# Per-head KV column tiles, `wo` folded in 32x32 tiles, re-paced first keys, and later modulation rows spread through DRAM, in an adaLN block with linear attention and SwiGLU

## The chip, the cores and the metric

The kernel runs on one core of one Trainium2 chip. The metric is the device time of one execution in microseconds (us). The engines: PE is TensorE's matmul, PEld its weight load, DVE is VectorE, ACT is ScalarE, POOL is GpSimd, SPq is the queue of SyncE.

## The reference, cut to what matters

```python
x = A_x                                            # [1, 2048, 1024] bf16
mod = (silu(c) @ w_mod).reshape(1, 6, 1, -1)       # six rows of 1024
sa, ca, ga, sb, cb, gb = mod[:, 0], ..., mod[:, 5]
h = layernorm(x) * (1 + ca) + sa
# attention: q, k, v = h @ wqkv, 32 heads of 32; pq, pk = phi(q), phi(k)
kv = einsum('bhsd,bhse->bhde', pk, v);  z = sum_s pk
o = (pq @ kv) / (pq . z + 1e-6)                    # per head
x = x + ga * (o @ wo)
h = layernorm(x) * (1 + cb) + sb
x = x + gb * ((silu(h @ w_gate) * (h @ w_up)) @ w_down)   # 1024 -> 3584 -> 1024
```

## The kernel before

The sequence is cut in four chunks (`sc`) of 512 rows. Per chunk TensorE makes keys, values and queries from `hT`, the transposed and modulated layernorm. The products of keys and values (KV) are summed over the chunks, and then each head's 32x32 block of KV is multiplied into `wo` ("folded"), so that queries need only one product. All this is the first 185 us; gate/up and down follow.

```python
def mm(out, lhsT, rhs, start, stop):       # lhsT is loaded as weights, rhs moves
    return tc.keep_in_program_order(nc.tensor.matmul(out, lhsT=lhsT, rhs=rhs, start=start, stop=stop))
def keep_warm(acc, n):                     # filler matmuls on zeros, for the clock
    for _ in range(n):
        mm(acc[:], lhsT=sel[:, 0, :], rhs=sel[:], start=True, stop=True)

def kv_phase(sc):                          # four heads at once: 128x128, off-diagonal blocks masked later
    for hg0 in range(0, HG, 3):
        ...
            for t in range(STC):
                mm(kvv[:, i, :], lhsT=pks[sc][:, t, (hg0 + i) * P:(hg0 + i + 1) * P],
                   rhs=vs[sc][:, t, hg0 + i, 0:P + 1], start=(t == 0), stop=(t == STC - 1))
        ... # vector: copy or add into kv_acc

def mod_rows(blks):                        # rows ga, gb (chunk 2) or sb, cb (chunk 3): 32 matmuls in four column tiles
    ...
def mod_bc(row):                           # chunk 2: spread ga, gb over the partitions
    for g in range(4):
        mm(ps[:], lhsT=sel[:, g, :], rhs=row[:], start=True, stop=True); ...
def mod_cols(row):                         # chunk 3: sb, cb as columns
    ... # 16 matmuls of one column

# first keys of chunk 0 (b: half of the columns, q=1: scale ca, q=0: shift sa)
pe_transpose_tile(hT, xns[0], 0, DC);  keep_warm(spare, 1)
mod_block(0, 1, 0, 4)
pe_transpose_tile(hT, xns[1], 1, DC);  keep_warm(spare, 1)
pe_transpose_tile(hT, xns[2], 2, DC // 2);  keep_warm(spare, 3)
mod_block(0, 0, 0, 2)
...                                        # modulate, mod_block(0, 0, 2, 4), modulate
k_mms(0, gs, accs, 0, 3)
...
k_mms(0, gs7, accs7, 0, 4)
mod_block(1, 0, 0, 2)
for cc in (4, 5): modulate(hT, cc, ca1T, saT)

# the fold, spread between query groups
for hg, nb in wf[3 * (qc - 5):3 * (qc - 4)]:
    ps = acc_b("wf")
    w = wo[hg // 4][:, hg % 4, nb * NB:(nb + 1) * NB]
    mm(ps[:], lhsT=KVT[:, hg, :], rhs=w, start=True, stop=True)
    nc.scalar.copy(out=w, in_=ps[:])
```

## Time and profile before

| | before |
|---|---|
| first timing, median of 3 | 844.36 us |
| span of the profile | 841.5 us |
| PE busy | 833.8 us, 99% |
| KV phase, four of them | 1.81 us each (1.91 ahead of the rows) |
| KV transposes | 0.54 us |
| broadcast (`bcr`) and column (`mcol`) matmuls of the later rows | 0.87 and 0.41 us |

From the page of the kernel before: the busy table's line of PE, the row of the granted clock in tenths over 40 slices, and the chain of work that ended last.

```profile
PE 833.8 (99%) x4289; PEld 385.5 (46%) x4289; DVE 306.8 (36%) x599; ACT 176.2 (21%) x268; POOL 55.6 (7%) x163
...
PEclk9999999999999999999999999999999999999999
...
PE 98%; DMA 1%; SPq 0%; DVE 0%; issue 0%
```

TensorE is what there is to shorten. Its waits, all of them (view of waits, PE: total us, times, longest):

```profile
PE mod_ps L98 <- DMA wme<-in_w_mod_dram: 1.8, 1, 1.8
PE acc L98 <- DVE sel L412: 1.2, 1, 1.2
PE acc L98 <- DVE hT L221: 0.7, 1, 0.7
PE mod_ps L98 <- DVE saT L267: 0.2, 1, 0.2
```

The timeline of PE in the kernel before (start us, busy us, line, tiles, shapes, count). A matmul's busy time includes its latency (379 ns for 512 columns, which start 216 ns apart), so a group's cost is the distance from its start to the start of the next line.

```profile
14.78 4.06 PE L98 MATMUL acc<-wk,hT 128*128 128x512 bf16 x18
...
31.86 13.98 PE L98 MATMUL acc<-wv,hT 128*128 128x512 bf16 x64
...
62.94 1.98 PE L98 MATMUL kvp<-v,pk 128*128 128x129 bf16 x32
64.75 10.52 PE L98 MATMUL acc<-wk,hT 128*128 128x512 bf16 x48
...
161.69 0.61 PE L101 MATMUL tp<-ident,kvs 128*128 128x128 bf16 x8
162.23 0.63 PE L98 MATMUL den<-pq,Zden 128*32 128x128 bf16 x32
...
166.25 0.81 PE L98 MATMUL wf<-wo,kvs 128*128 128x512 bf16 x3
...
183.52 13.98 PE L98 MATMUL a_ps<-wo,pq 128*128 128x512 bf16 x64
```

The `den` line is the model for what the change does to KV: "128*32" is a matmul in a column tile of 32, and 32 of them, each of 128 moving columns, need 0.56 us.

### The profile page before, as it was taken

The page shows a single profiled execution, that of the slowest core. Times are in us where ns is not written, and L with a number is a line of the kernel's source. Part 1 is how long each engine was busy: PE and PEld are TensorE (multiplying, and loading weights), DVE is VectorE, ACT ScalarE, POOL GpSimd, SP SyncE. Part 2 cuts the span into 40 slices and gives each one's busy share as a digit, 9 for nine tenths or more (in the row PEclk, how much of TensorE's full clock was granted, in tenths as well). Part 3 has the DMA queues.
Part 4 walks back from the last instruction along what each step waited for, and adds up shares of the span by engine and source line. Part 5 has one row for each costly group of instructions (what it writes and reads, how often), then busy time and mean ns, then how long its engine had stood idle before and what let it go on. Part 6 is the DMA issues. An engine that isn't in the chain of part 4 may idle for free.

```text
span 841.5 us, 10528 instructions
## 1 busy us (share of the span) xinstructions
PE 833.8 (99%) x4289; PEld 385.5 (46%) x4289; DVE 306.8 (36%) x599; ACT 176.2 (21%) x268; POOL 55.6 (7%) x163
## 2 busy tenths in 40 slices
PE   8999999999999999999999999999999999999998
PEld 4444444544444444444444444444444444444444
DVE  5656563467523324432221344211124432111122
ACT  3355353354211111101111010111110101111000
POOL 3011010112050001100000010000001100000000
PEclk9999999999999999999999999999999999999999
DMA  9895770029998545528434073581504629720011
GB/s 304 308 248 122 232 188 1 2 52 250 348 236 251 193 145 175 154 70 257 151 100 150 25 233 106 178 260 52 198 1 131 182 69 315 238 66 1 17 60 50
DMA packets 127232, 128.74 MB, mean 153 GB/s; under 512 B 33616, under 2 KB 108880, under 8 KB 126672
## 3 DMA queue, kind: packets, MB, share of 16 engines
q1 hardware_dynamic: 123600, 115.36, 45.7%
q0 software_dynamic: 3584, 12.72, 4.9%
q8 instruction: 33, 0.54, 0.3%
q14 instruction: 15, 0.12, 0.1%
HBM read 108.01 MB, written 12.71 MB: 143 GB/s over the span
## 4 chain that ended last, share of the span: by engine, by line
PE 98%; DMA 1%; SPq 0%; DVE 0%; issue 0%
PE acc L98 89%; PE a_ps L98 7%; DMA wme<-in_w_mod_dram 1%; PE kvp L98 1%; PE modr L98 0%; PE wf L98 0%; PE mod_ps L98 0%; PE den L98 0%; SPq L120 0%; PE tp L101 0%; PE bcr L98 0%; SPq L131 0%; SPq L125 0%; DVE hT L221 0%; PE mcol L98 0%
## 5 line engine op out<-in xcount | busy, mean ns | idle before, releaser
L98 PE MATMUL acc<-h2T,wgu 128*128 128x512 bf16 x1792 | 387.6, 379 | 0.0
L98 PEld LDWEIGHTS <-wgu 128*128 128x128 bf16 x1792 | 175.0, 98 | 211.6
L98 PE MATMUL acc<-wd,gu 128*128 128x512 bf16 (+2 forms) x924 | 196.1, 373 | 0.0
L591 DVE TENSOR_TENSOR gu<-acc,e 128x512 bf16<-128x512 f32 x112 | 77.5, 692 | 299.3 <-PE acc L98 296.5
L590 ACT ACTIVATE e<-acc 128x512 f32<-128x512 f32 x112 | 66.9, 597 | 374.8 <-PE acc L98 374.8
L98 PEld LDWEIGHTS <-gu 128*128 128x128 bf16 x924 | 89.2, 98 | 104.6
L98 PEld LDWEIGHTS <-hT 128*128 128x128 bf16 x512 | 49.4, 98 | 60.3 <-DVE hT L221 1.3
L612 DVE TENSOR_TENSOR e<-acc,gb_bc 128x512 f32<-128x512 f32 (+2 forms) x33 | 22.3, 676 | 131.3 <-PE acc L98 131.3
L98 PE MATMUL acc<-wk,hT 128*128 128x512 bf16 x256 | 57.6, 379 | 0.7 <-DVE hT L221 0.7
L98 PE MATMUL a_ps<-wo,pq 128*128 128x512 bf16 x256 | 57.4, 379 | 0.0
L98 PE MATMUL acc<-hT,wq 128*128 128x512 bf16 x256 | 57.1, 379 | 0.0
L98 PE MATMUL acc<-wv,hT 128*128 128x512 bf16 x256 | 55.9, 379 | 0.0
L273 ACT ACTIVATE eb<-acc 128x512 bf16<-128x512 f32 x64 | 37.9, 596 | 63.4 <-PE acc L98 60.3
L218 ACT ACTIVATE xn<-x,nmr,rstd 128x1024 bf16<-128x1024 f32 x16 | 19.8, 1240 | 126.3 <-POOL nmr L216 126.3
L274 DVE TENSOR_SCALAR eb<-eb 128x512 bf16<-128x512 bf16 x64 | 18.4, 291 | 58.7 <-ACT eb L273 58.6
L98 PEld LDWEIGHTS <-pq 128*128 128x128 bf16 x256 | 25.0, 98 | 30.3
L98 PEld LDWEIGHTS <-wq 128*128 128x128 bf16 x256 | 24.9, 98 | 29.8
L559 POOL DMA_DIRECT2D x_scratch<-x x16 | 9.6, 600 | 418.6 <-DVE x L552 418.6
L552 DVE TENSOR_TENSOR x<-a_ps,x_sb 128x512 f32<-128x512 f32 x32 | 22.1, 692 | 8.2 <-PE a_ps L98 8.1
L202 POOL TENSOR_TENSOR rstd<-veps,neg_half 128x1 f32<-128x1 f32 x32 | 18.0, 562 | 86.0 <-DVE veps L200 75.2
L311 ACT CAST v<-acc 128x512 bf16<-128x512 f32 x32 | 18.3, 582 | 22.0 <-PE acc L98 22.0
L615 DVE TENSOR_TENSOR ob<-e,x1r 128x512 bf16<-128x512 f32 (+2 forms) x33 | 22.3, 675 | 1.0
(72 smaller groups left out, 276.9 us busy)
## 6 DMA issues: line engine op xcount, KB each, us to landing
wgu<-in_B_w_gate_dram SPq DMA_DIRECT2D x28, 1024.0 KB, 7.5
wgu<-in_B_w_up_dram SPq DMA_DIRECT2D x28, 1024.0 KB, 8.7
x_sb<-in_A_x_dram SPq DMA_DIRECT2D x32, 256.0 KB, 6.7
wml<-in_w_mod_dram SPq DMA_DIRECT2D x8, 1024.0 KB, 8.6
x_scratch<-x POOLq DMA_DIRECT2D x16, 512.0 KB, 3.1
x1r<-x_scratch SPq DMA_DIRECT2D x31, 256.0 KB, 2.9
wd<-in_B_w_down_dram SPq DMA_DIRECT2D x7, 1024.0 KB, 5.6
rbc<-rden_scratch POOLq DMA_DIRECT2D x16, 256.0 KB, 5.2
```

The source lines that it names most:

```text
L98: return tc.keep_in_program_order(nc.tensor.matmul(out, lhsT=lhsT, rhs=rhs, start=start, stop=stop))
L202: nc.gpsimd.tensor_tensor(out=rstd[:, 0:n], in0=veps[:, 0:n], in1=neg_half[:].to_broadcast([P, n]), op=ALU.pow)
L218: nc.scalar.activation(out=dst, in_=src, func=ACT.Identity, bias=nmr[:], scale=rstd[:, 0:1])
L273: nc.scalar.activation(out=e[:], in_=acc, func=ACT.Exp)
L274: nc.vector.tensor_scalar(out=e[:], in0=e[:], scalar1=1.0, scalar2=PHI_EPS, op0=ALU.min, op1=ALU.add)
L311: nc.scalar.copy(out=v[:, t, nb * 4:(nb + 1) * 4, 0:P], in_=acc[:].rearrange("p (g e) -> p g e", e=P))
L552: nc.vector.tensor_tensor(out=x1[:, ns], in0=a_ps[:], in1=x_t[:, ns], op=ALU.add)
L559: nc.gpsimd.dma_start(out=x1_dram[st * P:(st + 1) * P, :], in_=x1[:])
L590: nc.scalar.activation(out=sg[:], in_=ps[0][:], func=ACT.Silu)
L591: gm = nc.vector.tensor_tensor(out=guT[sc][f // GPT][:, f % GPT, :], in0=ps[1][:], in1=sg[:], op=ALU.mult)
L612: nc.vector.tensor_tensor(out=yt, in0=y_ps, in1=gb_bc[:, ns], op=ALU.mult)
L615: nc.vector.tensor_tensor(out=ob, in0=yt, in1=x1r, op=ALU.add)
```

## The change

Intent: do the KV products per head, in column tiles of 32, four of which work side by side; fold `wo` with 16 tiles of 32x32 at once; take the spreading of the later modulation rows off TensorE; and re-pace the first keys so that TensorE waits less for the modulation.

```diff
 def kv_phase(sc):
-    ... # 8 groups x 4 row tiles, 128x128, 129 columns
+    kvp = acc_b("kvp", (HG, 2, DH))
+    for hg in range(HG):
+        for t in range(STC):
+            for i in range(HPC):
+                mm(kvp[i * DH:(i + 1) * DH, hg, :, :], lhsT=pks[sc][:, t, hg * P + i * DH:hg * P + (i + 1) * DH],
+                   rhs=v_ones(vs[sc], t * D + hg * P + i * DH), start=(t == 0), stop=(t == STC - 1))
   (v_ones: the head's 32 columns of v, then 32 ones; the masks kvmask and KVZ go)

+    def fold_wo(h, nb):
+        ps = [acc_b("wf") for _ in range(4)]           # all four PSUM buffers of the pool
+        for i in range(HPC):
+            for g in range(4):
+                mm(ps[g][i * DH:(i + 1) * DH, :], lhsT=KVT[rs, h, i * DH:(i + 1) * DH], rhs=wo[h][rs, i, ns], ...)
+        for g in range(4):
+            (nc.scalar.copy if g % 2 == 0 else nc.vector.tensor_copy)(out=wo[h][:, g, ns], in_=ps[g][:])
+    q_phase(1, 4, 6);  fold_wo(0, 0)
+    q_phase(1, 6, 8);  fold_wo(0, 1)
+    q_phase(2, 0, 2);  fold_wo(1, 0)
+    q_phase(2, 2, 3);  fold_wo(1, 1)
   (wo is loaded in another layout, 8 loads instead of 2; KV transposes 2 instead of 8)

-    mod_bc(row), mod_cols(row)
+    def mod_spread(k, row):
+        for g in range(4):
+            nc.gpsimd.dma_start(out=mrow_dram[k, g:g + 1, :], in_=row[32 * g:32 * g + 1, :])
+        if k == 0: ...      # two broadcast loads from DRAM into ga_bc and gb_bc
+        else: ...           # one load of 2048 single elements, then sbT and cb1T on vector
   (chunks 2 and 3: the rows' matmuls now stand behind two more key groups)

 # first keys
-    mod_block(0, 1, 0, 4)                       # moved behind the second transpose
     pe_transpose_tile(hT, xns[1], 1, DC); keep_warm(spare, 1)
+    mod_block(0, 1, 0, 4)
...
-    mod_block(0, 0, 0, 2) / (0, 0, 2, 4)
+    mod_block(0, 0, 0, 1) / (0, 0, 1, 4)
...
-    k_mms(0, gs7, accs7, 0, 4)
+    k_mms(0, gs7, accs7, 0, 2)
     mod_block(1, 0, 0, 2)
     for cc in (4, 5): modulate(hT, cc, ca1T, saT)
+    k_mms(0, gs7, accs7, 2, 4)
```

More of the change, by code (lines that the diff above doesn't have):

```diff
@@ L53 @@
     FPB = FBW // P
-    VW = P + 2
+    VT = STC * D
     GPT = 8
@@ L61 @@
     wqkv_v = A_wqkv.rearrange("(c p) n -> p c n", p=P)
-    wo_v = A_wo.rearrange("(c p) n -> p c n", p=P)
+    wo_v = A_wo.rearrange("(h g i e) n -> h g e i n", h=2, g=4, i=HPC)
     wg_v = B_w_gate.rearrange("(c p) f -> p c f", p=P)
@@ L178 @@
     gb_bc = const.tile([P, D], BF16, name="gb_bc")
-    kvs = k8.tile([P, HG * VW + HG * P], F32, name="kvs", tag="k8")
-    kv_acc = kvs[:, 0:HG * VW].rearrange("p (g e) -> p g e", e=VW)
-    kvb = kvs[:, HG * VW:].bitcast(BF16).rearrange("p (k g e) -> p k g e", k=2, e=P)
-    KVZ, KVT = kvb[:, 0], kvb[:, 1]
+    kvs = k8.tile([P, HG * (2 * DH + 1)], F32, name="kvs", tag="k8")
+    kv_acc = kvs[:, 0:HG * (DH + 1)].rearrange("p (g e) -> p g e", e=DH + 1)
+    kvb = kvs[:, HG * (DH + 1):].bitcast(BF16)
+    KVB = kvb[:, 0:HG * DH].rearrange("p (g e) -> p g e", e=DH)
+    KVT = kvb[:, HG * DH:].rearrange("p (h e) -> p h e", e=P)
     Zden = const.tile([P, HG, DH], BF16, name="Zden")
-    kvmask = const.tile([P, P], BF16, name="kvmask")
     zmask = const.tile([P, HG, DH], BF16, name="zmask")
@@ L188, in build_masks @@
     def build_masks():
-        nc.gpsimd.memset(kvmask[:], 0.0)
         nc.gpsimd.memset(zmask[:], 0.0)
@@ L192, in build_masks @@
             rs = slice(h * DH, (h + 1) * DH)
-            nc.gpsimd.memset(kvmask[rs, rs], 1.0)
             for hg in range(HG):
                 nc.gpsimd.memset(zmask[rs, hg, HG * h + hg:HG * h + hg + 1], 1.0)
-            nc.gpsimd.memset(sel[h * DH:h * DH + 1, h, :], 1.0)
     def rstd_of(mv, n):
@@ L300, in v_phase @@
     def v_phase(sc):
-        v = big("v", [STC, HG, VW])
+        v = big("v", [VT + DH])
         vs[sc] = v
-        nc.gpsimd.memset(v[:, :, :, P:VW], 1.0)
+        nc.gpsimd.memset(v[:, VT:], 1.0)
         for t in range(STC):
@@ L310, in v_phase @@
                                      start=(cc == 0), stop=(cc == DC - 1))
-                nc.scalar.copy(out=v[:, t, nb * 4:(nb + 1) * 4, 0:P], in_=acc[:].rearrange("p (g e) -> p g e", e=P))
+                nc.scalar.copy(out=v[:, t * D + nb * NB:t * D + (nb + 1) * NB], in_=acc[:])
     def q_phase(sc, lo=0, hi=DC):
@@ L321, in q_phase, with v_ones @@
             phi_to(pqs[sc][:, qc, :], acc[:])
+    def v_ones(v, lo):
+        head = v[:, lo:lo + DH]
+        return bass.AP(head.tensor, head.offset, [list(head.ap[0]), [VT - lo, 2], [1, DH]])
     def kv_phase(sc):
-        for hg0 in range(0, HG, 3):
-            nh = min(3, HG - hg0)
-            kvp = acc_b("kvp")
-            kvv = kvp[:, 0:3 * (P + 1)].rearrange("p (g e) -> p g e", e=P + 1)
-            for i in range(nh):
-                for t in range(STC):
-                    mm(kvv[:, i, :], lhsT=pks[sc][:, t, (hg0 + i) * P:(hg0 + i + 1) * P],
-                                     rhs=vs[sc][:, t, hg0 + i, 0:P + 1], start=(t == 0), stop=(t == STC - 1))
-            dst = kv_acc[:, hg0:hg0 + nh, 0:P + 1]
-            if sc == 0:
-                nc.vector.tensor_copy(out=dst, in_=kvv[:, 0:nh, :])
-            else:
-                nc.vector.tensor_tensor(out=dst, in0=dst, in1=kvv[:, 0:nh, :], op=ALU.add)
+        kvp = acc_b("kvp", (HG, 2, DH))
[4 more added lines that the diff above has]
+                       rhs=v_ones(vs[sc], t * D + hg * P + i * DH), start=(t == 0), stop=(t == STC - 1))
+        kvv = kvp[:].rearrange("p g k e -> p g (k e)")[:, :, 0:DH + 1]
+        if sc == 0:
+            nc.vector.tensor_copy(out=kv_acc, in_=kvv)
+        else:
+            nc.vector.tensor_tensor(out=kv_acc, in0=kv_acc, in1=kvv, op=ALU.add)
     def mod_load(cols):
@@ L354, in mod_rows @@
         return row
-    def mod_bc(row):
+    mrow_dram = dram.tile([2, 4, NB], BF16, name="mrow_scratch")
+    def mod_spread(k, row):
         for g in range(4):
-            ps = acc_b("bcr")
-            mm(ps[:], lhsT=sel[:, g, :], rhs=row[:], start=True, stop=True)
-            dst = (ga_bc if g < 2 else gb_bc)[:, (g % 2) * NB:(g % 2 + 1) * NB]
-            nc.scalar.copy(out=dst, in_=ps[:])
-    def mod_cols(row):
-        ps = acc_b("mcol")
-        for g in range(4):
-            for i in range(4):
-                mm(ps[:, g * 4 + i:g * 4 + i + 1], lhsT=row[:, i * P:(i + 1) * P], rhs=sel[:, g, 0:1],
-                                 start=True, stop=True)
-        nc.vector.tensor_copy(out=sbT[:], in_=ps[:, 0:DC])
-        nc.vector.tensor_scalar_add(out=cb1T[:], in0=ps[:, DC:2 * DC], scalar1=1.0)
+            nc.gpsimd.dma_start(out=mrow_dram[k, g:g + 1, :], in_=row[32 * g:32 * g + 1, :])
+        if k == 0:
+            for dst, g in ((ga_bc, 0), (gb_bc[:], 2)):
+                src = mrow_dram[0, g:g + 2, :].rearrange("g n -> (g n)").unsqueeze(0).to_broadcast([P, D])
+                nc.gpsimd.dma_start(out=dst, in_=src)
+        else:
+            cols = small.tile([P, 2 * DC], BF16, name="mcol", bufs=1)
+            with nc.allow_non_contiguous_dma(reason="2048 elements, once"):
+                nc.gpsimd.dma_start(out=cols[:], in_=mrow_dram[1].rearrange("g (i p) -> p (g i)", p=P))
+            nc.vector.tensor_copy(out=sbT[:], in_=cols[:, 0:DC])
+            nc.vector.tensor_scalar_add(out=cb1T[:], in0=cols[:, DC:2 * DC], scalar1=1.0)
     def modulate_all(hT, scaleT, biasT):
@@ L430 @@
         keep_warm(spare, 1)
-        mod_block(0, 1, 0, 4)
         pe_transpose_tile(hT, xns[1], 1, DC)
         keep_warm(spare, 1)
+        mod_block(0, 1, 0, 4)
         pe_transpose_tile(hT, xns[2], 2, DC // 2)
         keep_warm(spare, 3)
-        mod_block(0, 0, 0, 2)
-        for cc in (0, 1):
-            modulate(hT, cc, ca1T, saT, 0, H)
-        mod_block(0, 0, 2, 4)
-        for cc in (2, 3):
-            modulate(hT, cc, ca1T, saT, 0, H)
+        for lo, hi in ((0, 1), (1, 4)):
+            mod_block(0, 0, lo, hi)
+            for cc in range(lo, hi):
+                modulate(hT, cc, ca1T, saT, 0, H)
         k_mms(0, gs, accs, 0, 3)
@@ L474 @@
             kv_phase(sc - 1)
+            k_phase(sc, 2, 4)
             if sc >= 2:
-                row = mod_rows(blks)
-            k_phase(sc, 2, 4)
-            if sc == 2:
-                mod_bc(row)
-            if sc == 3:
-                mod_cols(row)
+                mod_spread(sc - 2, mod_rows(blks))
             k_phase(sc, 4, 8)
@@ L501 @@
         if sc == 2:
-            wo = load_w(wo_v, 0, "wo")
+            wo = [big("wo", [4, D]) for _ in range(2)]
+            for h in range(2):
+                for g in range(4):
+                    nc.sync.dma_start(out=wo[h][g * DH:(g + 1) * DH, :, :], in_=wo_v[h, g])
             for cc in range(DC):
@@ L508 @@
     kv_phase(NSC - 1)
-    for h in range(2):
-        hs = slice(4 * h, 4 * h + 4)
-        nc.vector.tensor_tensor(out=KVZ[:, hs, :], in0=kv_acc[:, hs, 0:P],
-                                in1=kvmask[:].unsqueeze(1).to_broadcast([P, 4, P]), op=ALU.mult)
-        nc.vector.tensor_tensor(out=Zden[:, hs, :], in0=kv_acc[:, hs, P:P + 1].to_broadcast([P, 4, DH]),
-                                in1=zmask[:, hs, :], op=ALU.mult)
-    q_phase(1, 2, 4)
-    tpk = acc_b("tp", (HG, P), BF16)
-    for hg in range(HG):
-        transpose(tpk[:, hg, :], KVZ[:, hg, :])
-    nc.scalar.copy(out=KVT[:, 0:4, :], in_=tpk[:, 0:4, :])
-    nc.vector.tensor_copy(out=KVT[:, 4:8, :], in_=tpk[:, 4:8, :])
+    nc.vector.tensor_copy(out=KVB, in_=kv_acc[:, :, 0:DH])
+    nc.vector.tensor_tensor(out=Zden[:], in0=kv_acc[:, :, DH:DH + 1].to_broadcast([P, HG, DH]),
+                            in1=zmask[:], op=ALU.mult)
+    q_phase(1, 2, 4)
+    tpk = acc_b("tp", (2, P), BF16)
+    for h in range(2):
+        transpose(tpk[:, h, :], KVB[:, 4 * h:4 * h + 4, :].rearrange("p g e -> p (g e)"))
+    nc.vector.tensor_copy(out=KVT, in_=tpk[:])
     den_sum(0)
     den_spread(0)
-    q_phase(1, 4, 5)
-    wf = [(hg, nb) for hg in range(HG) for nb in range(NNB)]
-    for qc in range(5, 11):
-        q_phase(1 + qc // 8, qc % 8, qc % 8 + 1)
-        for hg, nb in wf[3 * (qc - 5):3 * (qc - 4)]:
-            ps = acc_b("wf")
-            w = wo[hg // 4][:, hg % 4, nb * NB:(nb + 1) * NB]
-            mm(ps[:], lhsT=KVT[:, hg, :], rhs=w, start=True, stop=True)
-            nc.scalar.copy(out=w, in_=ps[:])
+    def fold_wo(h, nb):
+        ns = slice(nb * NB, (nb + 1) * NB)
+        ps = [acc_b("wf") for _ in range(4)]
+        for i in range(HPC):
+            for g in range(4):
+                rs = slice(g * DH, (g + 1) * DH)
+                mm(ps[g][i * DH:(i + 1) * DH, :], lhsT=KVT[rs, h, i * DH:(i + 1) * DH], rhs=wo[h][rs, i, ns],
+                   start=True, stop=True)
+        for g in range(4):
+            (nc.scalar.copy if g % 2 == 0 else nc.vector.tensor_copy)(out=wo[h][:, g, ns], in_=ps[g][:])
+    q_phase(1, 4, 6)
+    fold_wo(0, 0)
+    q_phase(1, 6, 8)
+    fold_wo(0, 1)
+    q_phase(2, 0, 2)
+    fold_wo(1, 0)
+    q_phase(2, 2, 3)
+    fold_wo(1, 1)
     h2Ts = {}
```

## The prediction

> **What bounds it now.** TensorE: the busy table has PE at 833.8 of 841.5 us, its clock row is at 9 tenths throughout, and the chain of work that ended last is 98% PE. PE's waits: 1.8 us (w_mod columns), 1.2 (start), 0.7 (a modulated hT), 0.2. Gate/up and down are untouched; only the first 185 us can shrink.
>
> **What changes on PE**, costed as the distance from a group's first matmul to the next group's (PE timeline):
>
> 1. KV products. Now 4 phases of 32 full matmuls of 129 columns, 1.81 us each. After: 512 matmuls of 32x64, four column tiles side by side. The trace has such tiles: the 32-column denominators (128 moving columns) start in fours 3 to 4 ns apart, one four every 56 ns, with about 0.1 us lost on entering and leaving; the Trainium skill, "TensorEngine Tiling (Array Packing)", Key Properties, says a mode switch drains, and this trace agrees. At 64 columns I estimate 34 ns a four: 1.3 us a phase. Gain 2.3 us; if a four still takes 56 ns, none.
> 2. Folding wo. Now 16 matmuls, 3.5 us. After: 4 folds of 16 tiles of 32x32x512. "TensorE: Matmul & The Clock Gate", Part 3, measured 10.6x for such a pack; no tile of this kind is in this trace. Estimate 0.46 us a fold (216 ns, staggers, two switches): gain 1.6 us. But a fold needs all four PSUM buffers of its pool, and before the last fold lies one query group only (1.73 us), while the previous fold's VectorE copies queue behind a phi (which ends 1.85 us after its matmuls' slot; then two copies of about 0.65): estimated PE stall 0.9 us. Net 0.7.
> 3. KV transposes: 8 become 2, gain 0.4.
> 4. Later modulation rows: the 4 broadcast (0.87 us) and 16 column matmuls (0.41) go: gain 1.3.
> 5. First keys: two key columns of group 7 now fill part of the 0.7 us wait for hT: gain 0.4. Moving the first block behind the second transpose gains nothing: the next w_mod columns land at 13.5 us.
>
> **New hazard.** The sb/cb columns come through DRAM as 2048 elements of 2 bytes, and VectorE waits for them in order, ahead of the eighth phi(k) of the last chunk. Small writes took 1.3 us from issue to first packet; packets of 4 and 16 bytes took 9 ns; I estimate a landing 8 to 10 us after the row copy. PE has four key and three value groups (12 us) before it needs that buffer: most likely no stall, at worst 2 to 3 us.
>
> **Sum:** 2.3 + 0.7 + 0.4 + 1.3 + 0.4 = 5.1 us, nearly all on the chain. Predicted 839.4 us, 8 in 10 between 837.0 and 842.4. Faster by over 2%: 0.01; within 2%: 0.98; slower by over 2%: 0.01.
>
> **What would show it.** KV phases of 1.2 to 1.4 us, fours 30 to 40 ns apart; folds of 0.4 to 0.5 us; a PE wait of about 0.9 us at the last fold; no bcr or mcol matmuls; the hT wait near 0.3 us; VectorE waiting for mcol without PE waiting then. From 185 us on, the same slots, earlier.
>
> **What would make it wrong.** Tiles of 64 columns bound by weight loads; the 16 tiles not running together (a fold of 1 us); mcol or wo landing late; a stall in the feed-forward part from shifted DMAs.

## The result, and the profile after

| | before | after |
|---|---|---|
| median of 4 runs | 844.27 us | 839.06 us (838.13 to 840.47) |
| ratio | | 0.9938 (0.9921 to 0.9955) |
| span of the profile | 841.5 us | 837.2 us |
| mean clock in the profile | 1.0 | 0.998 |

The time predicted was 839.4 us.

From the page after, the same lines:

```profile
PE 830.1 (99%) x4695; PEld 380.1 (45%) x4695; DVE 307.2 (37%) x597; ACT 169.9 (20%) x255; POOL 60.7 (7%) x165
...
PEclk9999999999999999999999999999999999999999
...
PE 98%; DMA 1%; DVE 0%; SPq 0%; issue 0%; ACT 0%
```

PE's waits after:

```profile
PE acc L98 <- DVE sel L411: 1.2, 1, 1.2
PE mod_ps L98 <- DMA wme<-in_w_mod_dram: 1.1, 2, 0.9
PE tp L101 <- ACT xn L215: 0.9, 2, 0.6
...
PE acc L98 <- DVE hT L218: 0.2, 1, 0.2
PE wf L98 <- DVE wo L526: 0.2, 1, 0.2
```

The wait for hT fell from 0.7 to 0.2 us as forecast, and a wait for VectorE at `wf` appeared. PE's timeline after:

```profile
14.42 5.73 PE L98 MATMUL acc<-wk,hT 128*128 128x512 bf16 x18
...
32.59 13.98 PE L98 MATMUL acc<-wv,hT 128*128 128x512 bf16 x64
...
63.77 1.22 PE L98 MATMUL kvp<-v,pk 128*32 128x64 bf16 x128
64.92 10.53 PE L98 MATMUL acc<-wk,hT 128*128 128x512 bf16 x48
...
158.93 0.28 PE L101 MATMUL tp<-ident,kvs 128*128 128x128 bf16 x2
159.14 0.63 PE L98 MATMUL den<-pq,Zden 128*32 128x128 bf16 x32
...
171.10 0.43 PE L98 MATMUL wf<-wo,kvs 32*32 32x512 bf16 x16
171.47 1.90 PE L98 MATMUL acc<-hT,wq 128*128 128x512 bf16 x8
173.30 0.58 PE L98 MATMUL wf<-wo,kvs 32*32 32x512 bf16 x3
174.11 0.43 PE L98 MATMUL wf<-wo,kvs 32*32 32x512 bf16 x13 [0.23 <-DVE wo L526]
174.47 5.35 PE L98 MATMUL acc<-hT,wq 128*128 128x512 bf16 x24
179.66 13.98 PE L98 MATMUL a_ps<-wo,pq 128*128 128x512 bf16 x64
```

A KV phase takes 64.92 - 63.77 = 1.15 us instead of 1.81. A fold takes 171.47 - 171.10 = 0.37 us, the last one 174.47 - 173.30 = 1.17 us. The stall in the last fold is 0.8 us, although its wait line says only 0.2: each matmul behind the gap has its own wait, and the busy time of the three before it covers most of the gap.

One line goes the other way. The same 18 first key matmuls take 5.73 us instead of 4.06, and the values start at 32.59 us instead of 31.86. The table of stretches tells why. Its columns: the stretch in us, its length, then busy us and instructions of PE, PEld, DVE, ACT and POOL, then the granted clock, the DMA share and GB/s. First the kernel before:

```profile
11.00:15.00 4.00, 3.62 (x79) 2.71 (x77) 2.10 (x7) 0.58 (x1) 0.00 (x0) 1.00 1.05 378
15.00:18.40 3.40, 3.40 (x17) 1.56 (x16) 2.63 (x9) 0.00 (x0) 0.89 (x4) 1.00 1.14 339
```

and the changed kernel:

```profile
11.00:15.00 4.00, 2.88 (x56) 1.92 (x53) 1.49 (x6) 0.58 (x1) 0.00 (x0) 1.00 1.05 378
15.00:18.40 3.40, 3.40 (x10) 1.22 (x8) 2.67 (x8) 0.00 (x0) 0.89 (x5) 0.50 1.11 341
```

The clock is halved from 15 to 18.4 us: the trace's clock record has one stretch of 3.413 us at 0.5. In it matmuls of 512 columns start 427 ns apart instead of 216. The Trainium skill, "TensorE: Matmul & The Clock Gate", Part 1, describes this: a gate judges TensorE's activity in windows of 3413 ns and grants half the clock after an idle one. The length agrees to the nanosecond. But the 3.41 us before the half clock were not idle here: TensorE was busy for 2.29 us of them (11.55 to 14.96 us). The page's row of tenths cannot show it, since a slice of 21 us with 3.4 us at half speed still rounds to 9.

Slot by slot, from the two timelines (distance between the same landmarks):

| slot | before | after | difference |
|---|---|---|---|
| start to the values of chunk 0 | 31.86 | 32.59 | +0.73 |
| two key groups and KV, chunk 1 | 5.27 | 4.70 | -0.57 |
| chunk 2: keys, KV, rows and their spread | 18.44 | 17.02 | -1.42 |
| chunk 3: the same | 17.97 | 17.02 | -0.95 |
| query groups and KV, last | 8.72 | 8.16 | -0.56 |
| KV transposes | 0.54 | 0.21 | -0.33 |
| denominators to the first output tile, with the folds | 21.29 | 20.52 | -0.77 |

The sum is -3.87, and the first output tile starts 183.52 - 179.66 = 3.86 us earlier; from there both kernels keep the same pace until their last VectorE instruction. The rest of the 4.3 us between the spans, 0.4 us, lies behind that instruction.

### The profile page after: what moved, and what is told of

It reads as the page before. It is cut to its first block, busy times and chain, and to the rows that moved or that the text cites. A ratio compares the mean times of both kernels' runs of the same rounds, so it can differ in the third digit from the quotient of the medians.

```text
span 837.2 us, 11341 instructions
## 1 busy us (share of the span) xinstructions
PE 830.1 (99%) x4695; PEld 380.1 (45%) x4695; DVE 307.2 (37%) x597; ACT 169.9 (20%) x255; POOL 60.7 (7%) x165
## 4 chain that ended last, share of the span: by engine, by line
PE 98%; DMA 1%; DVE 0%; SPq 0%; issue 0%; ACT 0%
PE acc L98 89%; PE a_ps L98 7%; DMA wme<-in_w_mod_dram 1%; PE kvp L98 1%; PE modr L98 0%; PE mod_ps L98 0%; PE den L98 0%; SPq L120 0%; DVE wo L526 0%; PE wf L98 0%; DVE pq L273 0%; SPq L131 0%; ACT eb L270 0%; PE tp L101 0%; SPq L125 0%
## 5 line engine op out<-in xcount | busy, mean ns | idle before, releaser
L98 PE MATMUL acc<-wk,hT 128*128 128x512 bf16 x256 | 59.5, 387 | 0.3 <-DVE hT L218 0.2
L199 POOL TENSOR_TENSOR rstd<-veps,neg_half 128x1 f32<-128x1 f32 x32 | 17.9, 559 | 74.9 <-DVE veps L197 72.6
```

Of the source, the lines that this page charges most:

```text
L199: nc.gpsimd.tensor_tensor(out=rstd[:, 0:n], in0=veps[:, 0:n], in1=neg_half[:].to_broadcast([P, n]), op=ALU.pow)
```

## The experiments

Three batches, each on one chip, with runs of the kernel before beside them. "Full clock" is a run whose mean clock is printed as 1.0, "low" one of 0.998 or less; a single half-clock stretch of 3.4 us is worth 0.002.

| kernel | median us | ratio to before (95%) | runs | full clock, mean us | low, mean us |
|---|---|---|---|---|---|
| before, all three batches | | | 33 | 20, 842.88 | 8, 844.92 |
| warm_fill | 838.67 | 0.9946 (0.9932 to 0.9961) | 6 | 3, 837.79 | 2, 840.04 |
| keys_old | 839.44 | 0.9955 (0.9943 to 0.9967) | 6 | 1, 838.22 | 5, 839.67 |
| split_only | 837.32 | 0.9941 (0.9924 to 0.9957) | 6 | 4, 837.14 | 2, 839.77 |
| keys_only | 843.17 | 1.0002 (0.9988 to 1.0015) | 6 | 3, 842.55 | 3, 844.20 |
| after_again | 839.26 | 0.9949 (0.9932 to 0.9965) | 6 | 2, 837.53 | 4, 839.61 |
| warm_all | 837.88 | 0.9937 (0.9924 to 0.9950) | 5 | 5, 837.81 | 0 |
| fold_early | 838.45 | 0.9940 (0.9924 to 0.9956) | 6 | 2, 836.44 | 4, 838.86 |
| rows_next | 839.83 | 0.9961 (0.9947 to 0.9976) | 6 | 1, 840.01 | 5, 839.84 |
| rows_on_pe | 839.16 | 0.9949 (0.9935 to 0.9962) | 6 | 3, 838.36 | 3, 840.03 |
| warm_early | 836.92 | 0.9922 (0.9910 to 0.9934) | 6 | 6, 836.97 | 0 |

(Runs missing from both columns had 0.999. kv_narrow is told below; its result is wrong.)

### First batch: is the new key order what halves the clock?

**warm_fill**, more filler in one place:

```diff
         pe_transpose_tile(hT, xns[2], 2, DC // 2)
-        keep_warm(spare, 3)
+        keep_warm(spare, 7)
```

> The changed kernel with seven instead of three filler matmuls before it waits for the second w_mod block (13.2 us). Theory (the clock is halved because TensorE was too little busy around 11.5 to 15 us): the clock row stays at full speed, the first 18 key matmuls take about 4.1 us instead of 5.7, the first value matmul starts near 30.9 us instead of 32.6, time 1.5 us below the changed kernel. Rival (the key matmuls are slowed by loads or SBUF traffic): the filler changes nothing, 18 matmuls still take 5.7 us, the time is within 0.3 us of the changed kernel.

**keys_old**: the changed kernel with the old order of all first keys.

```diff
+        mod_block(0, 1, 0, 4)
         pe_transpose_tile(hT, xns[1], 1, DC);  keep_warm(spare, 1)
-        mod_block(0, 1, 0, 4)
-        mod_block(0, 0, 0, 1) ... mod_block(0, 0, 1, 4)
+        mod_block(0, 0, 0, 2) ... mod_block(0, 0, 2, 4)
-        k_mms(0, gs7, accs7, 0, 2) ... k_mms(0, gs7, accs7, 2, 4)
+        k_mms(0, gs7, accs7, 0, 4)
```

> The changed kernel with the whole order of the first keys as before. Theory: full clock again, value matmuls start near 31.6 to 31.9 us, about 0.8 us faster than the changed kernel. Rival (the slow keys come from something else in the change, such as the masks that are no longer set): the 18 key matmuls stay near 5.7 us.

**split_only**: as keys_old, but group 7's keys stay split around the third block.

```diff
-        k_mms(0, gs7, accs7, 0, 4)
+        k_mms(0, gs7, accs7, 0, 2) ... k_mms(0, gs7, accs7, 2, 4)
```

> The changed kernel with the first modulation blocks ordered as before, but group 7's keys still split around the third block. Theory: full clock, the wait for hT near 0.3 us, value matmuls start near 31.3 us, 0.4 us better than keys_old and about 1.2 us better than the changed kernel. Rival (the split is worth nothing, the wait only moves): equal to keys_old.

**keys_only**: the kernel before with the new order alone (the reverse of keys_old's diff).

> The kernel before with only the new order of the first keys. Theory: the clock halves for about 3.4 us near 15 us as in the changed kernel, value matmuls start near 32.6 us, 0.7 us slower than the kernel before. Rival (the new order is a gain of 0.4 us as predicted, and the slow clock belongs to another part of the change): full clock, 0.4 to 1 us faster than the kernel before.

Measured. All four profiles happened to fall in runs at full clock; in all four the first key matmuls take 4.0 to 4.1 us. In the other runs the clock is mixed. The new order on the kernel before (keys_only) has full clock in three runs of six, and the old order in the changed kernel (keys_old) is low in five of six. So the theory that the new order decides over the clock fell. What stands: the half clock comes in some runs and not in others, in every one of these kernels, and costs about 2 us when it comes (1.4 to 2.6 us between the two columns of the table). The rival, slow keys by traffic, fell too: at full clock they are not slow, with the same loads running. Filler in one wait alone (warm_fill) is not enough: two of its six runs are low.

What the order itself is worth can be read at full clock. The split does what it should; PE's timelines of keys_old and then of split_only:

```profile
22.46 2.55 PE L98 MATMUL acc<-wk,hT 128*128 128x512 bf16 x11 [0.70 <-DVE hT L218]
```

```profile
22.05 2.55 PE L98 MATMUL acc<-wk,hT 128*128 128x512 bf16 x11 [0.25 <-DVE hT L218]
```

The wait falls by 0.45 us. The whole new order is worth little: keys_only's full-clock runs average 842.55 us against 842.81 for the kernel before in that batch, and over all runs the ratio is 1.0002.

### Second batch: does filler hold the clock, and where are the other losses?

**after_again** is the changed kernel itself.

> The changed kernel itself once more, to be beside the others of this batch. Theory as it now stands (the half clock is a matter of chance: one 3.4 us stretch at half clock shows as a mean clock of 0.998 and costs 1.7 us, two as 0.996): its runs show a mixture of mean clocks 1.0, 0.998 and 0.996, and its time rises by about 1.7 us from one to the next. Rival (the new key order always brings the half clock): every run at 0.998 or less.

**warm_all**: filler in every early wait.

```diff
-    keep_warm(spare, 20)
+    keep_warm(spare, 21)
...
         pe_transpose_tile(hT, xns[0], 0, DC)
-        keep_warm(spare, 1)
+        keep_warm(spare, 4)
         pe_transpose_tile(hT, xns[1], 1, DC)
-        keep_warm(spare, 1)
+        keep_warm(spare, 2)
         mod_block(0, 1, 0, 4)
         pe_transpose_tile(hT, xns[2], 2, DC // 2)
-        keep_warm(spare, 3)
+        keep_warm(spare, 6)
...
             mod_block(0, 0, lo, hi)
+            keep_warm(spare, 1)
```

> The changed kernel with filler matmuls in every wait of the first 14 us (21, 4, 2, 6 instead of 20, 1, 1, 3, and one in the wait for the shift columns). Theory (the stretch from 7 to 15 us is too little busy, and the half clock comes or not with the place of the window): at most one run of six below a mean clock of 0.999, median 1 us below after_again, at equal clock the same time within 0.3 us. Rival (the filler does not count, or the half clock comes from elsewhere, 20 to 26 us): the clocks are mixed as in after_again.

after_again is low in four runs of six; with the four runs of the first result the changed kernel is low in eight of ten. One half-clock stretch costs 2.1 us here (839.61 against 837.53), not 1.7, and the one run at 0.996 took no longer than those at 0.998, so the second step that I expected of a further stretch was not there. warm_all has full clock in all five runs, and they lie within 0.5 us of each other. Nothing was changed but filler in the first 15 us, and warm_early below holds the clock with it too: none of eleven runs is low, against eight of ten without. So filler there keeps the half clock away: it comes of a TensorE too little busy in those 15 us. At equal clock warm_all is not faster than after_again (837.81 and 837.53): one filler too many stands behind the last shift columns, and the first keys wait for it.

Not settled is why the changed kernel loses the clock more often (8 of 10) than the kernel before (8 of 33): keys_old, whose TensorE order up to the values is that of the kernel before, is low as often as the changed kernel. In the four profiles of low runs (the changed kernel, after_again, fold_early, rows_on_pe) the stretch starts at 14.5 to 15.6 us, 10.24 us behind the clock record's first entry, so it is always the fourth window.

The kept traces allow one step more. Count windows of 3.413 us from the first entry of each profile's clock record: in the third window, the one before the stretch in question, TensorE is busy for 2.21 to 2.42 us in the four low profiles, and for 2.48 to 3.18 us in the eight at full clock that have a record (those of the first batch lack a few matmul records, so they are if anything higher). kv_narrow and rows_next, with the same early code as the changed kernel, are among the eight (2.48 and 2.55 us); their first entry lies at 6.1 us from the start, those of the four low profiles, which all have that early code, at 4.3 to 5.4 us. So the place of the window matters, as warm_all's theory had it. A threshold on busy time alone does not follow: fold_early's second window has only 1.67 us, and full clock behind it.

**fold_early**: each fold one query group earlier.

```diff
-    q_phase(1, 4, 6);  fold_wo(0, 0)
-    q_phase(1, 6, 8);  fold_wo(0, 1)
-    q_phase(2, 0, 2);  fold_wo(1, 0)
-    q_phase(2, 2, 3);  fold_wo(1, 1)
+    q_phase(1, 4, 5);  fold_wo(0, 0)
+    q_phase(1, 5, 7);  fold_wo(0, 1)
+    q_phase(1, 7, 8);  q_phase(2, 0, 1);  fold_wo(1, 0)
+    q_phase(2, 1, 3);  fold_wo(1, 1)
```

> The changed kernel with the four folds one query group earlier, so that two groups stand before each, the last one too. Theory (the last fold waits for VectorE, which copies two banks of the fold before behind a phi): the last fold's slot falls from 1.17 us to about 0.37 us as the other three, no wait of wf for VectorE, time 0.8 us below the changed kernel at equal clock. Rival (the stall moves: the first fold then waits for its PSUM buffers or KVT): a first fold of 1 us and no gain.

PE's timeline of fold_early, the last fold:

```profile
173.80 0.43 PE L98 MATMUL wf<-wo,kvs 32*32 32x512 bf16 x16
174.17 5.35 PE L98 MATMUL acc<-hT,wq 128*128 128x512 bf16 x24
```

The last fold takes 0.37 us, no fold waits, and at full clock the kernel is 1.1 us faster than after_again (836.44 against 837.53, two runs each), at low clock 0.75 us (838.86 against 839.61, four each); from the denominators to the first output tile the trace has 179.36 - 159.64 = 19.72 us instead of 20.52. The median hides it behind the clock.

**rows_next**: the rows' matmuls directly behind the KV products.

```diff
             kv_phase(sc - 1)
-            k_phase(sc, 2, 4)
             if sc >= 2:
                 mod_spread(sc - 2, mod_rows(blks))
+            k_phase(sc, 2, 4)
```

> The changed kernel with the later modulation rows again directly behind the KV products instead of behind two more key groups. Theory (entering and leaving the four column tiles costs about 0.1 us each, and both groups use the same tiling): KV and rows together take 0.2 us less in each of two chunks, 0.4 us in all, and nothing else moves. Rival (the two key groups were put between because TensorE would wait there, for w_mod columns or for the buffers of the row's spread): a wait at modr, or a later one, and no gain.

The saving is there: KV takes 92.67 - 91.64 = 1.03 us instead of 1.15, as both groups use the same tiling. But the rival was right, and not by the wait that it named. PE's timeline of rows_next, in chunk 2:

```profile
91.64 1.22 PE L98 MATMUL kvp<-v,pk 128*32 128x64 bf16 x128
92.67 1.92 PE L98 MATMUL modr<-wml,sc 128*32 128x512 bf16 x32
...
109.29 10.52 PE L98 MATMUL acc<-wv,hT 128*128 128x512 bf16 x48 [0.78 <-DVE pk L273]
```

GpSimd's timeline of the same run shows where that wait begins:

```profile
95.59 2.16 POOL L359 DMA_DIRECT2D mrow_scratch<-mrow  x4 [15.78 <-ACT mrow L352]
97.74 0.14 POOL L300 MEMSET v<- 128x32 bf16 x1
103.82 0.57 POOL L363 DMA_DIRECT2D e<-mrow_scratch  x1 [5.93 <-DMA mrow_scratch<-mrow]
104.38 0.56 POOL L363 DMA_DIRECT2D gb_bc<-mrow_scratch  x1
104.95 0.58 POOL L199 TENSOR_TENSOR rstd<-veps,neg_half 128x1 f32<-128x1 f32 x1
```

GpSimd takes its instructions in the order of the program in this trace. It has to wait until the four rows have landed in DRAM before it may issue the broadcast loads (the Trainium skill, "DMA: Bandwidth & Descriptors", "Two DMAs through the same engine are not ordered", says that only the completion semaphore orders them), and here that wait is 5.93 us. The layernorm's `rstd` of chunk 3 stands behind it; ScalarE waits for it 3.69 us with an exponential of the keys behind; and PE waits for that key's buffer. In the changed kernel two `rstd` stand ahead of the loads, and the same wait is 0.64 us. Its GpSimd timeline:

```profile
100.29 2.16 POOL L359 DMA_DIRECT2D mrow_scratch<-mrow  x4 [0.84 <-ACT mrow L352]
...
104.90 0.69 POOL L363 DMA_DIRECT2D e<-mrow_scratch  x1 [0.64 <-DMA mrow_scratch<-mrow]
```

The order explains at most the 1.8 us (102.47 to 104.27) that the `rstd` and their `nmr` fill. The rows also landed later: from the first issue to the first load it is 103.82 - 95.59 = 8.23 us in rows_next and 104.90 - 100.29 = 4.61 here; the slowest row needed 7.0 us from issue to landing against 3.9. In rows_next their first packet moved 4.1 us after the first issue, while the DMA engines still moved 174 to 349 GB/s for other loads; in the changed kernel 1.3 us after, with that traffic ending (19 GB/s from 102.5 to 104.9 us). That the traffic held the rows up fits, and was not tested alone. From the keys of chunk 2 to the last queries rows_next needs 150.53 - 88.09 = 62.44 us, the changed kernel 150.77 - 89.11 = 61.66.

### Third batch: what bounds a KV tile, what the spread is worth, and both finds together

**kv_narrow**: 33 moving columns instead of 64.

```diff
-  mm(kvp[i * DH:(i + 1) * DH, hg, :, :], lhsT=..., rhs=v_ones(vs[sc], t * D + hg * P + i * DH), ...)
+  mm(kvp[i * DH:(i + 1) * DH, hg, 0:DH + 1], lhsT=..., rhs=vs[sc][:, lo:lo + DH + 1], ...)
   (lo: the head's first column of v)
```

> The changed kernel with 33 moving columns in a KV tile instead of 64: the 32 of the head and the next column of v in place of the ones, so z and the result are wrong on purpose. In the changed kernel the first ten fours of a KV phase start 29 ns apart and the others 33 ns. Theory A (the moving columns bound a four: 64 at full clock are 27 ns plus 2.5): fours 16 to 20 ns apart, a phase of 0.7 to 0.8 us instead of 1.15. Theory B (the rate at which pairs of weight load and matmul reach the array bounds it, 8.3 ns a pair): fours still about 33 ns apart after the first ten, a phase of 1.1 us. Between them: the first ten at 16 to 20 ns, the rest at 33.

PE's timeline of kv_narrow:

```profile
62.80 1.20 PE L98 MATMUL kvp<-v,pk 128*32 128x33 bf16 x128
63.93 10.53 PE L98 MATMUL acc<-wk,hT 128*128 128x512 bf16 x48
```

(The 27 and 2.5 ns of theory A are an estimate from spacings in these traces: 216 ns for 512 columns and 56 ns for 128 make 0.42 ns a column and some 2.6 ns besides.) A phase takes 1.13 us against 1.15: halving the columns gains almost nothing. The two runs, both at full clock, took 837.94 and 837.53 us; those of after_again have a mean of 837.53 (other chip). By the matmuls' start times the fours behind the first start 25 to 26 ns apart for the next seven (29 to 30 ns for some ten in the changed kernel), and from then on 33 ns apart in both, with single matmuls 8 to 9 ns apart instead of in bunches. So the columns do not bind the bulk of a phase; pairs of weight load and matmul come every 8.3 ns there. What sets that rate, the feeding of instructions or the weight loads, no run separates; that the first fours, loads included, come every 25 ns speaks against the loads. That the first fours go faster because a queue is filled while TensorE drains for the new mode fits, but was not shown.

**rows_on_pe**: the spread back on TensorE, in the places of the kernel before.

```diff
             kv_phase(sc - 1)
-            k_phase(sc, 2, 4)
             if sc >= 2:
-                mod_spread(sc - 2, mod_rows(blks))
+                row = mod_rows(blks)
+            k_phase(sc, 2, 4)
+            if sc == 2: mod_bc(row)
+            if sc == 3: mod_cols(row)
   (mod_bc, mod_cols and the four memsets of sel come back as they were)
```

> The changed kernel with the later modulation rows spread by TensorE again (rows, four broadcast and sixteen column matmuls in the places they had before). Theory: the broadcast slot is 0.87 us and the column slot 0.41 us again, the two mode switches at the rows are saved (0.1 us each chunk), time about 1.1 us above the changed kernel at equal clock, GpSimd and VectorE do not wait for the spread. Rival (the spread through DRAM gives back part of what it saves in waits elsewhere): less than 0.6 us above.

By its timeline the two spreads take 0.86 and 0.40 us, but chunks 2 and 3 together only 0.84 us more than in the changed kernel (62.50 against 61.66 from the keys of chunk 2 to the last queries). The difference is the placing: directly behind KV, the rows save the switches of tiling, 0.2 us a chunk and twice what I had put down. At full clock it is 0.8 us slower than after_again (838.36 against 837.53), at low clock 0.4 us (840.03 against 839.61), on another chip. The timeline's 0.84 us lies between the two expectations: the spread through DRAM is worth about 0.8 us, not 1.3, since its rows stand apart from KV.

**warm_early**: fold_early and the filler of warm_all, without its last one.

> Both finds together: fillers in the early waits (21, 4, 2, 6, and one only behind the first shift column) and the folds one query group earlier. Theory: every run at a mean clock of 1.0, the last fold 0.37 us, median 836.5 to 837.2 us, 5.5 to 6 us below the kernel before and 2 us below the median of the changed kernel. Rival: one of the two finds loses its effect beside the other, median 837.8 us or more.

```diff
   (fold_early's diff, and warm_all's with)
-            keep_warm(spare, 1)
+            keep_warm(spare, 1 if lo == 0 else 0)
```

PE's waits in warm_early, all of them:

```profile
PE acc L98 <- DVE sel L411: 1.2, 1, 1.2
PE mod_ps L98 <- DMA wme<-in_w_mod_dram: 0.3, 1, 0.3
PE acc L98 <- DVE hT L218: 0.2, 1, 0.2
PE tp L101 <- DVE xn L209: 0.2, 1, 0.2
```

It has full clock in all six runs and a median of 836.92 us, a ratio of 0.9922 to the kernel before; the result is correct. It has the lowest median of all, but at full clock it is not faster than fold_early (836.97 against 836.44, two runs, other chip): what the filler buys is the clock. The clock record of its profile is empty, which prints as 1.0; its key matmuls start 215 to 216 ns apart from 14.3 to 17.9 us, so the clock was full there. With warm_all, filler held the clock in eleven runs of eleven.

## Why the prediction was right

The time was 839.06 us where 839.4 was forecast, and most terms of the sum hold.

1. KV products: forecast 2.3 us. The four slots give 2.2 (0.57 + 0.55 + 0.54 + 0.56, the middle ones being -1.42 and -0.95 less the 0.87 and 0.41 us of the spread; if the spread is credited only with the 0.84 us of rows_on_pe, KV gets 2.7). Fours start 29, then 33 ns apart; 34 was forecast. The reason given was half wrong: the columns do not set the later ones, kv_narrow shows; what does set them, instructions or weight loads, stays open.
2. The fold: forecast 0.7 net, measured 0.77 over its stretch. A fold takes 0.37 us (0.46 forecast), the switch of tiling adds 0.1 us ahead of each, and the last fold stalls 0.8 us (0.9 forecast) for the reason given; fold_early takes the stall away by giving it the second query group.
3. KV transposes: forecast 0.4, measured 0.33.
4. Later rows: forecast 1.3, the time of the 20 matmuls. They are gone, but rows_on_pe shows the spread through DRAM to be worth 0.84 us: the prediction left out that the rows move away from KV and that two more switches of tiling come in.
5. First keys: forecast a gain of 0.4. The wait for hT fell from 0.7 to 0.2 us. But the profile shows this part 0.73 us longer, because the clock was halved for 3.4 us, which costs half of that, 1.7 us: the step that failed is the silent one, that the clock stays at full speed as it did in the profile before. At full clock the whole new order gains 0.3 us (keys_only), within what few runs can tell.

The new hazard was named and judged right: VectorE waits 2.3 us for the sb/cb columns, and PE does not wait then. The landing, at 139.4 us, came 8.5 us after the end of the row copy (130.3 + 0.6), in the forecast 8 to 10. The way there was not the one named: in the trace the load moves as 32 packets of 128 bytes of 0.09 to 0.31 us each, not as small ones of 9 ns. VectorE's line:

```profile
139.42 0.17 DVE L368 CAST sbT<-mcol 128x8 f32<-128x8 bf16 x1 [2.34 <-DMA mcol<-mrow_scratch]
```

But the more dangerous wait was another one, GpSimd's for the rows of the broadcast, and rows_next shows what it costs in a worse place.

At equal clock the change is worth 842.88 - 837.53 = 5.3 us (full) or 844.92 - 839.61 = 5.3 us (low); 5.1 was the sum. (The kernel before is taken from three chips, the changed one from two and four runs on one of them; on that chip alone it is 5.3 and 5.5.) The profiled pair shows less, 4.3 us, mainly because the clock was full in one and halved in the other, which by the trace costs 1.7 us. That would make 6.0 us; single runs at one clock spread by as much as that differs from 5.3.

That the medians came within 0.4 us of the forecast is in part luck. The spread was put 0.46 us too high and KV about as much too low, by the count that gives the spread its 0.84 us; and all four runs of the changed kernel were low, while the clocks of the four runs of the kernel before beside them are not on record.

## What to carry to other kernels

Where TensorE waits again and again at a kernel's start, fill the waits with matmuls on zeros even if no single wait is longer than 1 us: a lost window of clock cost about 2 us here, as much as all four KV slots gained, and it makes the timing of everything else noisy, so compare runs by their clock. Small matmuls in tiles are worth it until something other than the columns is the limit (here at 8.3 ns a pair of load and matmul); groups that use the same tiling belong next to each other. A spread through DRAM takes work off TensorE but puts a DMA round trip into the program of the engine that issues it: look at what stands behind that wait, and at what else the DMA engines move then, before you move it.

## What the Trainium skill lacked or had wrong

- "TensorE: Matmul & The Clock Gate", Part 1, HAM oscillation, gives the abstract rule as no idle gaps of TensorE over about 3.4 us. Here the clock was halved with no gap over 0.9 us in the 4 us ahead, TensorE being busy 2.88 us of them, and the matmuls among it mostly short. The page's next section tells of frequent short idle times that do the same, without a busy share. By the trace's own windows the low profiles had TensorE busy 2.21 to 2.42 us of 3.41, the full ones 2.48 to 3.18.
- The same page, Part 1, has start-to-start never below about 25 ns however small N is. That holds here for the one-column matmuls on the whole array (24 to 26 ns apart), not for column tiles: the matmuls of one four start 3 to 4 ns apart, as Part 3 has it for tiles, and single ones 8.3 ns apart over most of a KV phase, a rate that neither part has.
- "TensorEngine Tiling (Array Packing)", Key Properties, says that a mode switch drains TensorE but gives no cost. By the timelines it is about 0.1 us on entering and on leaving, and 0.2 us a chunk for rows placed apart from KV.
- "TensorE: Matmul & The Clock Gate", Part 3, gives 10.6x for 16 tiles of K = M = 32, N = 512, and does not say what a switch of tiling adds. Here such a fold spans 0.43 us and takes a slot of 0.37 us, 0.47 with the switch ahead of it; one after the other at 216 ns each the 16 would take 3.46 us (worked out), so 9.4x, or 7.4x with the switch.
- No page gives the time of a dependent pair, small rows written to DRAM and the load that reads them. From the first row's issue to the load's it was 4.61 us in one place and 8.23 us in another, with the same four rows.
